# One fused attention and mixture-of-experts kernel: no zero products ahead of the last row tiles of the first expert, its routing's next phase begun earlier, and half of its first weights asked for later

## The chip, the cores and the metric

The kernel runs on one core of a Trainium2 chip. The time is that of one execution on the device in microseconds (us). TensorE (PE) multiplies, VectorE (DVE) and ScalarE (ACT) work element by element, GpSimd (POOL) issues the transfers that gather and scatter rows, and SyncE (SP) issues the other transfers. All engines run side by side, each its own instructions in a fixed order, with semaphores between them.

## The reference

```python
scores = scale * q @ k.T            # 8 batches x 8 heads, 576 positions, 64 wide
scores = where((rel >= 0) & (rel < 128), scores + bias, -1e9)   # bias: -slope[head] * |rel|
x = softmax(scores) @ v             # -> x [4608, 512]

logits = x @ w_gate                 # 8 experts, cap = 4608 / 8 = 576 rows each
for idx in argsort(-logits.flatten()):     # greedy, best first
    tok, e = idx // 8, idx % 8
    if assigned[tok] < 0 and counts[e] < cap:
        assigned[tok] = e; counts[e] += 1
out[rows of e] = relu(x[rows of e] @ w1[e]) @ w2[e]     # w1 512x1024, w2 1024x512
```

Everything is float32. The greedy assignment orders all 36,864 logits, so which rows an expert gets depends on which experts are full already.

## The kernel before

**Attention** runs first and writes `x` to DRAM. During its last part the router begins.

**The router** (class `Router`) finds the assignment in phases 0 to 7. In each phase the expert that fills up first is determined with its 576 rows, by counting logits over thresholds: VectorE builds indicator matrices (`ind`), TensorE counts (L597, `m`), and after three such steps the number of the expert (`ei`, or `guess` in phase 0) and its rows (`idx`) come out, the latter through products at L744 and VectorE's L753. A phase begins with the best expert that is left for each row (`first_choice`, L504 to L511) and the range of the logits (`ends`, L518 to L548, with TensorE at L523 and L530). In the profile the router's phase 0 has the line L457. Each phase is a generator that stops at points where other work may be placed between.

In phase 0 the first 256 rows of the first expert (row tiles 0 and 1, `idxa`) are found ahead of the other 320 (row tiles 2 to 4, `idx`).

**An expert** has two layers in 5 row tiles (4 of 128, one of 64). Float32 products are made from parts: every operand is split into a high part, by a cast, and a low part, the rest, and three products (high·high, high·low, low·high) are added. The weights of a layer come as 4 chunks of 512 KB (`raw`, four buffers; `loads`, SP's queue, L987, behind a load of the expert's number into a register, L984), and `split` makes of each the high part on ScalarE (L994) and the low part in two instructions on VectorE (L996). Chunk c holds the columns of hidden blocks 2c and 2c+1 in layer 1, and the rows of these blocks in layer 2. The rows are gathered by GpSimd (`gather`, L1006), transposed by TensorE into a PSUM bank (`turn`, L1030; the pool of `pg` has one bank), and read out by ScalarE (`xh`, L1033) and VectorE (`xl`, L1034). Layer 1 is L1054 (`ph`), with relu on ScalarE (`hh`, L1060) and the low part on VectorE (`hlo`, L1065); layer 2 is L1082, L1083 and L1085 (`po`), read out at L1089, and GpSimd writes the rows out (L1094, from three buffers).

**The first expert** is handled ahead of the loop over the experts, in `layer_moe`: rows 0 to 255 through layer 1 (part 0) and layer 2 (tiles 0 and 1), and then rows 256 to 575 are gathered and turned, ahead of which and between which `keep_warm` puts 16, 4 and 4 products of zeros (L1014, 128x512, onto an idle bank), with the transposes of tiles 3 and 4 in banks of the pool `po`. Then the loop begins, with part 1 of layer 1 for the first expert.

**What sets the order.** Each engine's instructions are ordered ahead of time by a scheduler: what stands earlier in the program goes first where both could, except where the program holds an instruction behind another (`issue_after`) or keeps a row of them in the order of the program (`keep_in_program_order`). Inside the loop `slot(k, i)` is called between pieces of layer work and does what is due there: a step of the router, a load (table `W_LOAD`), a split (`W_SPLIT`), and from i = 16 on the gather and the turns of the next expert's rows.

Of the kernel before, what the change touches and what calls it, by code (L numbers as in the profile page):

```python
# [5 lines left out]
F32 = mybir.dt.float32  # L6
F32R = mybir.dt.float32r
BF = mybir.dt.bfloat16
I32 = mybir.dt.int32
# [6 lines left out]
E, DM, F, N = 8, 512, 1024, 4608  # L16
# [402 lines left out]

CONST_AT = 4  # L420
WARM, WARM0, WARM1 = 11, 16, 4
EARLY = 4
AHEAD = (18, 0, 0)
EARLY0 = 1
WARM_A = 8
W_LOAD = [(0, 1, 0, 0), (0, 1, 1, 2), (0, 1, 2, 6), (0, 1, 3, 10),
          (1, 0, 0, 13), (1, 0, 1, 16), (1, 0, 2, 19), (1, 0, 3, 22), (1, 1, 0, 28)]
W_SPLIT = [(0, 1, 0, 2), (0, 1, 1, 6), (0, 1, 2, 10), (0, 1, 3, 14),
# [11 lines left out]
AHEAD_COLS, AHEAD_ROWS = 28, 256  # L440
# [535 lines left out]
class MoE:  # L976
# [61 lines left out]
    def layer1(self, w1, xg, part=None):  # L1038
        nc = self.nc
# [5 lines left out]
        cut = (0, 288, 576) if part is None else (0, AHEAD_ROWS, 576)  # L1045
        order = [(f, (0, 1) if part is None else (part,)) for f in range(8)]
        for f, ts in order:
            w = w1[f // 2].rearrange("p a (j f) -> p a j f", j=4)
            fo = (f % 2) * 128
            pp = {t: self.p["ps_h"].tile([128, 512], F32, name="ph")[:, 0:cut[t + 1] - cut[t]] for t in ts}  # L1050
            for j in range(4):
                for a, x in ((0, xh), (0, xl), (1, xh)):
                    for t in ts:
                        nc.tensor.matmul(pp[t], w[:, a, j, fo:fo + 128], x[:, j, cut[t]:cut[t + 1]],  # L1054
                                         start=(j == 0 and a == 0 and x is xh), stop=(j == 3 and a == 1))
                if j == 1 and part != 0:
                    yield
# [86 lines left out]

def layer_moe(tc, P, C, r, m, exact):
    ei = r.ei[0] if exact else r.guess
    g = m.gather(r.idx[0], range(2), None if exact else m.x[0:128 * AHEAD_COLS, :])
    raw = list(m.loads(ei, 0))
    if not exact:
        with tc.issue_after(r.ahead_pe.ins):  # L1150
            m.idle = P["ps_h"].tile([128, 512], F32, name="ph")
            for _ in range(WARM_A):
                tc.nc.tensor.matmul(m.idle, C["zero"][:, 0:128], C["zero"], start=True, stop=True)
    W = {(0, 0): [m.split(raw[0])]}
    for _ in m.turn(g):
        pass
    W[0, 0] += [m.split(raw[c]) for c in range(1, 4)]
    second = list(m.loads(ei, 1))
    W[0, 1] = []
    for i, _ in enumerate(m.layer1(W[0, 0], m.xg, 0)):  # L1160
        if i % 2:
            W[0, 1].append(m.split(second[i // 2]))
    for _ in m.layer2(W[0, 1], m.h, r.idx[0], ts=range(2)):
        pass
    route = (n for k in range(1, E) for n in r.phase(k, exact))
    g = m.gather(r.idx[0], range(2, 5))
    with tc.issue_after(r.last.ins):
        for _ in range(EARLY0):
            next(route)
    with tc.issue_after(r.last_pe.ins):  # L1170
        m.idle = P["ps_h"].tile([128, 512], F32, name="ph")
        m.keep_warm(WARM0)
    tn = m.turn(g, True)
    next(tn)
    with tc.issue_after(m.turned.ins):
        late = P["rt"].tile([1, 1], I32, name="late")
        last = tc.nc.vector.tensor_copy(late, r.guess[0:1, 0:1])
    for _ in tn:
        pass
    with tc.issue_after(last.ins):  # L1180
        for _ in range(EARLY - EARLY0):
            next(route)
    st = dict(wait=0, turn=0)
    raws, loaders = {(0, 1): second}, {}

    def slot(k, i):

        st["wait"] -= 1
        if st["wait"] <= 0 and (k + 1 not in r.idx or k + 2 not in r.idx and i >= AHEAD[min(k, 2)]):
            st["wait"] = next(route, 0)  # L1190
        for e, layer, c, due in W_LOAD:
            e += k
            if i >= due and e in r.ei and len(raws.get((e, layer), ())) == c:
                if c == 0:
                    loaders[e, layer] = m.loads(r.ei[e], layer)
                    raws[e, layer], W[e, layer] = [], []
                raws[e, layer].append(next(loaders[e, layer]))
# [14 lines left out]
    for k in range(E):  # L1212
        i = 0
# [98 lines left out]
```

## Time and profile before

| what | us |
|---|---|
| median of 3 runs (lowest to highest) | 706.08 (705.92 to 706.16) |
| profiled execution, its own time | 703.26 |
| its span, first to last instruction | 701.5 |
| TensorE busy | 666.6 |
| VectorE busy | 457.0 |
| ScalarE busy | 326.1 |
| GpSimd busy | 152.8 |

The median is 0.2 to 0.4% above the profiled execution, which is a single one. In the profile, times of the trace count from the span's start. The attention ends at about 205; the first expert's layer 1 begins at 223.26, the turn of its row tiles 2 to 4 stands between 248.50 and 255.38, and the second expert's rows are turned from 290.86 on. A row of the timeline has start, length, engine, line, operation, output and inputs, and in brackets the idle time of the engine before it and what ended it.

### The profile page before, as it was taken

The numbers are of one execution on the slowest core, as the hardware profiler recorded it, in microseconds if no ns is written. First come the engines' busy times: TensorE is split into PE (matmuls) and PEld (weight loads), VectorE is DVE, ScalarE is ACT, GpSimd is POOL, SyncE is SP. The second block draws the span as 40 slices with busy tenths as digits, with TensorE's granted clock in tenths as the row PEclk, the third lists the DMA queues.
The fourth block names the chain that finished last, engine by engine and source line by source line (L and its number), as shares of the span: only waits on it lengthen the run. The fifth ranks groups of instructions, "written<-read, shape, count | busy, mean of one in ns | idle before, by whom it ended". The sixth has DMA issues, their size and how long they took to land.

```text
span 701.5 us, 18916 instructions
## 1 busy us (share of the span) xinstructions
PE 666.6 (95%) x7290; PEld 583.9 (83%) x7292; DVE 457.0 (65%) x1902; ACT 326.1 (46%) x992; POOL 152.8 (22%) x337
## 2 busy tenths in 40 slices
PE   8999999999956999699999999999999999999996
PEld 5899889989854977489779879889988988988985
DVE  6778887887878848679679829837855625423210
ACT  6998898988844212524233234224314324423211
POOL 4122222122311201403223141132133023011011
PEclk9999999999985999999999999999999999999998
DMA  8475756566327102706327235135135334301001
GB/s 300 158 226 175 223 184 222 185 223 192 104 68 271 39 30 66 272 9 203 136 91 255 70 105 173 61 122 171 53 121 159 108 110 136 121 30 39 1 24 49
DMA packets 35139, 92.72 MB, mean 132 GB/s; under 512 B 3808, under 2 KB 13152, under 8 KB 35040
## 3 DMA queue, kind: packets, MB, share of 16 engines
q1 hardware_dynamic: 29152, 72.55, 31.9%
q0 software_dynamic: 5888, 18.88, 8.2%
q8 instruction: 59, 0.97, 0.6%
q14 instruction: 40, 0.33, 0.1%
HBM read 72.54 MB, written 18.87 MB: 130 GB/s over the span
## 4 chain that ended last, share of the span: by engine, by line
PE 84%; DVE 9%; DMA 3%; ACT 2%; issue 2%; POOL 0%; POOLq 0%; SPq 0%; DVEq 0%
PE ph L1054 27%; PE po L1082 10%; PE po L1083 9%; PE po L1085 7%; PE x L53 7%; PE s L53 7%; PE pt L53 6%; PE pt L160 6%; PE pg L1030 2%; DVE hl L996 1%; DMA g<-x,idx 1%; DMA g<-x,idxa 1%; PE ph L1014 1%; ACT u L147 1%; PE m L597 1%
## 5 line engine op out<-in xcount | busy, mean ns | idle before, releaser
L1054 PE MATMUL ph<-xh,hl 128*128 128x288 f32 (+2 forms) x1024 | 193.1, 300 | 1.6 <-ACT xh L1033 1.6
L1054 PEld LDWEIGHTS ph<-xh,hl 128*128 128x128 f32 x1024 | 155.9, 190 | 3.3 <-ACT xh L1033 2.4
L1082 PE MATMUL po<-hl,hh 128*128 128x512 f32 (+1 forms) x328 | 131.4, 401 | 0.0
L1083 PE MATMUL po<-hl,hh 128*128 128x512 f32 (+1 forms) x328 | 127.7, 389 | 0.0
L147 ACT ACTIVATE u<-u,mn 128x192 f32<-128x192 f32 (+2 forms) x288 | 124.1, 438 | 5.3 <-DVE mn L137 5.2
L1054 PE MATMUL ph<-xl,hl 128*128 128x288 f32 (+2 forms) x512 | 117.1, 298 | 0.0
L1060 ACT ACTIVATE hh<-ph 128x288 fp32r<-128x288 f32 (+2 forms) x128 | 46.8, 408 | 144.3 <-PE ph L1054 144.2
L1085 PE MATMUL po<-hl,hlo 128*128 128x512 f32 (+1 forms) x264 | 101.9, 386 | 0.0
L996 DVE TENSOR_TENSOR hl<-raw,hl 128x512 fp32r<-128x512 f32 x128 | 85.4, 682 | 10.9 <-ACT hl L994 10.5
L137 DVE CUSTOM_DVE_ANT_0 u<-s,bm 128x192 f32<-128x192 f32 (+1 forms) x248 | 71.8, 345 | 30.1 <-PE s L53 29.5
L1054 PEld LDWEIGHTS ph<-xl,hl 128*128 128x128 f32 x512 | 85.0, 190 | 0.1
L1034 DVE TENSOR_TENSOR xl<-pg,xh 128x512 fp32r<-128x512 f32 (+1 forms) x38 | 24.4, 641 | 92.4 <-ACT xh L1033 92.2
L1094 POOL DMA_INDIRECT out_dram<-o,idx x38 | 42.1, 1108 | 191.5 <-ACT o L1089 115.5
L994 ACT CAST hl<-raw 128x1024 fp32r<-128x1024 f32 x64 | 65.5, 1047 | 21.5 <-DMA raw<-in_w_dram 14.3
L1065 DVE SCALAR_TENSOR_TENSOR hlo<-ph,hh 128x288 fp32r<-128x288 f32 (+2 forms) x128 | 50.0, 416 | 38.7 <-ACT hh L1060 38.3
L1082 PEld LDWEIGHTS po<-hl,hh 128*128 128x128 f32 x328 | 62.3, 190 | 11.2
L1083 PEld LDWEIGHTS po<-hl,hh 128*128 128x128 f32 x328 | 62.3, 190 | 11.0
L1089 ACT COPY o<-po 128x512 f32<-128x512 f32 (+1 forms) x33 | 18.9, 574 | 104.3 <-PE po L1085 74.3
L53 PE MATMUL s<-qk 64*64 64x192 f32 (+1 forms) x992 | 59.8, 325 | 1.0 <-DVE mn L137 0.9
L1006 POOL DMA_INDIRECT g<-x,idx x38 | 41.5, 1093 | 78.7 <-PE pg L1030 29.1
L1085 PEld LDWEIGHTS po<-hl,hlo 128*128 128x128 f32 x264 | 49.6, 188 | 10.1
L147 ACT ACTIVATION_READ_ACCUMULATOR u<-u,mn 128x1 f32 x288 | 56.0, 194 | 0.0
(260 smaller groups left out, 952.8 us busy)
## 6 DMA issues: line engine op xcount, KB each, us to landing
raw<-in_w_dram SPq DMA_DIRECT2D x64, 512.0 KB, 4.4
qk<-in_qk_dram SPq DMA_DIRECT2D x32, 576.0 KB, 5.0
v<-in_v_dram SPq DMA_DIRECT2D x32, 288.0 KB, 3.6
x<-xb SPq DMA_DIRECT2D x14, 512.0 KB, 3.6
x<-xb SPq DMA_DIRECT2D x8, 128.0 KB, 3.4
x<-xb SPq DMA_DIRECT2D x4, 256.0 KB, 2.2
g<-x,idx POOLq DMA_INDIRECT x38, 3.5
out_dram<-o,idx POOLq DMA_INDIRECT x38, 2.8
```

The source lines that it names most:

```text
L53: put(nc.tensor.matmul(out, w, a, start=start, stop=stop, skip_group_check=True))
L137: put(nc.vector.tensor_tensor_reduce(out=weights(n, t, h), in0=x[:, c:c + 64 * m].rearrange("q (j k) -> q j k", k=64), in1=bm[n % NP][:, y ...
L147: put(nc.scalar.activation(u, u, AF.Exp, bias=st["mn"][:, i:i + 1], scale=-1.0, accum_out=st["sm"][:, i:i + 1]))
L994: self.last = nc.scalar.copy(hl[:, 0, :], raw)
L996: nc.vector.tensor_tensor(hl[:, 1, c:c + 512], raw[:, c:c + 512], hl[:, 0, c:c + 512].bitcast(F32), ALU.subtract)
L1054: nc.tensor.matmul(pp[t], w[:, a, j, fo:fo + 128], x[:, j, cut[t]:cut[t + 1]], start=(j == 0 and a == 0 and x is xh), stop=(j == 3 and a = ...
L1060: nc.scalar.activation(o, pp[t], AF.Relu)
L1065: nc.vector.scalar_tensor_tensor(d, pp[t][:, c0:c1], 0.0, o[:, c0:c1].bitcast(F32), ALU.max, ALU.subtract)
L1082: nc.tensor.matmul(out, a, wh, start=(f == 0), stop=False)
L1083: nc.tensor.matmul(out, a, wl, start=False, stop=(f == 7 and t == 4))
L1085: nc.tensor.matmul(out, hl[:, f, 128 * t:128 * t + 128], wh, start=False, stop=(f == 7))
L1094: self.sent = nc.gpsimd.indirect_dma_start(out=self.out, out_offset=bass.IndirectOffsetOnAxis(ap=idx[t][:r], axis=0), in_=o[:r, :], in_off ...
```

## The change

- `EARLY`, the number of steps of phase 1 of the router that are issued ahead of the loop, goes from 4 to 3, and these steps now stand at the very beginning of `layer_moe`, without the `issue_after` that held them back. The first four slots of the first expert hold the router's step behind the last layer-1 product (`last_mm`), and `WAIT_B = 2` lets the first slot in the loop pass without one.
- Only two (`SOON`) of the four chunks of the first expert's layer-1 weights are asked for ahead of the gather of the first rows. The other two, and all four of layer 2, are asked for behind a copy of the expert's number (`late`) that VectorE makes after the first row tile's low part. On SP the queue so has a wait for VectorE between the second and the third chunk.
- The products of zeros ahead of and between the turns of row tiles 2 to 4 are gone, and all three tiles use the one bank `pg`. The 8 products of zeros at the start of the first expert (`WARM_A`) stay.

```diff
-EARLY = 4
+EARLY = 3
 AHEAD = (18, 0, 0)
-EARLY0 = 1
-WARM_A = 8
+WAIT_B = 2
+SOON, WARM_A = 2, 8
...
-                        nc.tensor.matmul(pp[t], w[:, a, j, fo:fo + 128], x[:, j, cut[t]:cut[t + 1]],
+                        self.last_mm = nc.tensor.matmul(pp[t], w[:, a, j, fo:fo + 128], x[:, j, cut[t]:cut[t + 1]],
...
     ei = r.ei[0] if exact else r.guess
-    g = m.gather(r.idx[0], range(2), None if exact else m.x[0:128 * AHEAD_COLS, :])
-    raw = list(m.loads(ei, 0))
+    route = (n for k in range(1, E) for n in r.phase(k, exact))
+    for _ in range(EARLY):
+        next(route)
+    raw = list(m.loads(ei, 0, range(SOON)))
+    ga = m.gather(r.idx[0], range(2), None if exact else m.x[0:128 * AHEAD_COLS, :])
...
-    W = {(0, 0): [m.split(raw[0])]}
-    for _ in m.turn(g):
+    W = {(0, 0): [m.split(raw[0])], (0, 1): []}
+    tn = m.turn(ga)
+    next(tn)
+    with tc.issue_after(m.turned.ins):
+        late = P["rt"].tile([1, 1], I32, name="late")
+        tc.nc.vector.tensor_copy(late, ei[0:1, 0:1])
+    raw += list(m.loads(late, 0, range(SOON, 4)))
+    for _ in tn:
         pass
     W[0, 0] += [m.split(raw[c]) for c in range(1, 4)]
-    second = list(m.loads(ei, 1))
-    W[0, 1] = []
+    second = list(m.loads(late, 1))
...
+    gb = m.gather(r.idx[0], range(2, 5))
     for _ in m.layer2(W[0, 1], m.h, r.idx[0], ts=range(2)):
         pass
-    route = (n for k in range(1, E) for n in r.phase(k, exact))
-    g = m.gather(r.idx[0], range(2, 5))
-    with tc.issue_after(r.last.ins):
-        for _ in range(EARLY0):
-            next(route)
-    with tc.issue_after(r.last_pe.ins):
-        m.idle = P["ps_h"].tile([128, 512], F32, name="ph")
-        m.keep_warm(WARM0)
-    tn = m.turn(g, True)
-    next(tn)
-    with tc.issue_after(m.turned.ins):
-        late = P["rt"].tile([1, 1], I32, name="late")
-        last = tc.nc.vector.tensor_copy(late, r.guess[0:1, 0:1])
-    for _ in tn:
+    for _ in m.turn(gb):
         pass
-    with tc.issue_after(last.ins):
-        for _ in range(EARLY - EARLY0):
-            next(route)
-    st = dict(wait=0, turn=0)
+    st = dict(wait=WAIT_B, turn=0)
...
         if st["wait"] <= 0 and (k + 1 not in r.idx or k + 2 not in r.idx and i >= AHEAD[min(k, 2)]):
-            st["wait"] = next(route, 0)
+            if k == 0 and i < 4:
+                with tc.issue_after(m.last_mm.ins):
+                    st["wait"] = next(route, 0)
+            else:
+                st["wait"] = next(route, 0)
```

What this does to the order of the instructions is shown at three places. The first is VectorE from phase 0's row indices (`idx`) on: `pen` to `L_72` end phase 0, L504 to L511 are the first choice of phase 1, and `hl<-raw,hl` is the low part of a weight chunk. Before:

```order
L457 TENSOR_SCALAR pen<-Dc 128x8
L1065 SCALAR_TENSOR_TENSOR hlo<-ph,hh 128x256
L457 TENSOR_TENSOR base<-pen,Dc 128x8
L457 SCALAR_TENSOR_TENSOR left<-keyv,kmx,left 128x8
L457 TENSOR_TENSOR L_4863<-L_sb,pen 128x288
L457 SCALAR_TENSOR_TENSOR L_72<-T_4787,L_4863 128x288
L457 TENSOR_REDUCE ov<-Dc 128x1
L504 TENSOR_REDUCE b<-L_72 128x36
```

And now, from `L_4863` on:

```order
L457 TENSOR_TENSOR L_4863<-L_sb,pen 128x288
L996 TENSOR_TENSOR hl<-raw,hl 128x512
L457 SCALAR_TENSOR_TENSOR L_72<-T_4787,L_4863 128x288
L457 TENSOR_REDUCE ov<-Dc 128x1
L996 TENSOR_TENSOR hl<-raw,hl 128x512
L457 TENSOR_SCALAR ov<-ov 128x1
L504 TENSOR_REDUCE b<-L_72 128x36
L457 SCALAR_TENSOR_TENSOR ov<-kmx,ov 128x1
L1065 SCALAR_TENSOR_TENSOR hlo<-ph,hh 128x256
```

Before, no low part of a chunk of the first expert stood behind phase 0's `idx`; now two stand here, and four more stand behind L511, between the small rows of phase 1's `ends`.

The second place is TensorE between the last layer-2 product of row tile 1 and part 1 of layer 1. Before, its end (16 products of zeros, the transposes of tile 2 and 4 more products of zeros are ahead of these rows):

```order
L1030 MATMUL po<-ident_sb,g 128x128 x4
L1014 LDWEIGHTS zero
L1014 MATMUL ph<-zero 128x512
L1014 LDWEIGHTS zero
L1014 MATMUL ph<-zero 128x512
L1014 LDWEIGHTS zero
L1014 MATMUL ph<-zero 128x512
L1014 LDWEIGHTS zero
L1014 MATMUL ph<-zero 128x512
L1030 MATMUL po<-ident_sb,g 128x64 x4
L523 MATMUL m<-ident_sb,ext 1x128
L1054 MATMUL ph<-xh,hl 128x320 x4
```

Now, the whole of it:

```order
L1085 MATMUL po<-hl,hlo 128x512
L1030 MATMUL pg<-ident_sb,g 128x128 x8
L1030 MATMUL pg<-ident_sb,g 128x64 x4
L1054 MATMUL ph<-xh,hl 128x320 x4
L1054 MATMUL ph<-xl,hl 128x320
```

The products of zeros are gone, the transposes of the three tiles follow each other into one bank, and phase 1's transpose (L523) has moved up into layer 2 of tiles 0 and 1. The first count of phase 1 (L597) stands behind 15 products of part 1 of layer 1, before behind 43.

The third place is TensorE where the second expert's rows are turned (L1030), among the layer-2 products of row tiles 2 to 4 of the first. The third and the fourth of the five turns, before:

```order
L1082 MATMUL po<-hl,hh 128x512
L1030 MATMUL pg<-ident_sb,g 128x128 x4
L1083 MATMUL po<-hl,hh 128x512
L1030 MATMUL pg<-ident_sb,g 128x128 x4
L1054 MATMUL ph<-xh,hl 128x288
L1030 MATMUL pg<-ident_sb,g 128x128 x4
L1054 MATMUL ph<-xl,hl 128x288
```

And now:

```order
L1030 MATMUL pg<-ident_sb,g 128x128 x4
L1082 MATMUL po<-hl,hh 128x512
L1083 MATMUL po<-hl,hh 128x512
L1082 MATMUL po<-hl,hh 128x512
L1083 MATMUL po<-hl,hh 128x512
L1054 MATMUL ph<-xh,hl 128x288
L1030 MATMUL pg<-ident_sb,g 128x128 x4
L1054 MATMUL ph<-xl,hl 128x288
```

The first turn stood behind 51 of the 64 layer-2 products of tiles 2 to 4 and stands behind 35 now; from each turn to the next there were 12, 1 and 0 of them, and now there are 13, 12 and 4. L744, the products that give the second expert's row indices, stood behind 30 layer-2 products and stands behind 16.

## The prediction

> **What bounds the kernel now.** I read the page first (the clock row and the chain that ended last), then busy time by stage, then the chain of waits where the products of zeros stand, then the timelines of TensorE, VectorE and GpSimd around the two places that the change touches. From the page:
>
> ```profile
> PEclk9999999999985999999999999999999999999998
> PE 84%; DVE 9%; DMA 3%; ACT 2%; issue 2%; POOL 0%; POOLq 0%; SPq 0%; DVEq 0%
> ```
>
> TensorE (PE) carries 84% of the chain, and its clock drops in one place of the 40, slices 13 and 14: between the attention and the first expert. What the change can win must be idle or slow time of PE. The stages around the first expert follow; after the two times of each stretch come its length, then busy time and count for PE, PE's weight loads, VectorE (DVE), ScalarE (ACT) and GpSimd (POOL), then granted clock, DMA share and GB/s.
>
> ```profile
> 205.00:223.26 18.26, 8.05 (x75) 4.94 (x76) 15.68 (x61) 6.64 (x9) 2.23 (x2) 0.53 0.65 224
> 223.26:237.40 14.14, 14.14 (x120) 13.73 (x120) 12.54 (x41) 5.80 (x11) 0.00 (x0) 0.88 0.21 75
> 237.40:248.50 11.10, 11.06 (x50) 8.94 (x50) 5.17 (x20) 0.98 (x3) 3.82 (x4) 1.00 0.28 83
> 248.50:255.38 6.88, 6.59 (x37) 3.49 (x36) 1.66 (x5) 2.12 (x4) 0.98 (x1) 1.00 0.11 40
> 255.38:272.10 16.72, 16.72 (x125) 15.45 (x126) 12.50 (x69) 3.06 (x7) 0.00 (x0) 1.00 0.00 0
> 272.10:286.90 14.80, 13.69 (x77) 9.88 (x75) 14.04 (x52) 5.73 (x8) 5.76 (x6) 1.00 0.66 222
> 286.90:290.86 3.96, 0.00 (x1) 0.01 (x1) 1.88 (x8) 1.01 (x1) 3.05 (x4) 1.00 0.80 248
> 290.86:303.50 12.64, 9.77 (x47) 7.46 (x48) 9.09 (x27) 5.97 (x9) 2.50 (x3) 0.86 0.40 141
> ```
>
> They are: the search for the first expert's rows; layer 1 on rows 0 to 255; layer 2 on row tiles 0 and 1; the turn of row tiles 2 to 4 with its products of zeros; layer 1 on the other rows, without a gap; layer 2 on row tiles 2 to 4; a standstill of PE; the hand-over to the second expert. Beyond 303.5 the order of the program is the same, so I shift the rest as a whole. Three stretches can change length: up to 248.5, 248.5 to 255.38, and 272 to 303.5.
>
> **Part 1: two chunks behind the first rows.** The first rows' gather goes out at 213.55. On PE, and by the DMA issues:
>
> ```profile
> 218.95 1.11 PE L1030 MATMUL pg<-ident_sb,g 128*128 128x128 f32 x4 [2.12 <-DMA g<-x,idxa]
> 223.26 0.79 PE L1054 MATMUL ph<-xh,hl 128*128 128x256 f32 x2 [0.68 <-ACT xh L1033]
> raw<-in_w_dram SPq DMA_DIRECT2D x8, 512.0 KB, 4.4
> g<-x,idxa POOLq DMA_INDIRECT x2, 5.4
> g<-x,idx POOLq DMA_INDIRECT x3, 3.4
> ```
>
> The first gathers take 5.4 us among four weight chunks; three later ones, with no weights in flight, take 3.4. With two chunks ahead I take the 3.4: the transposes and the first layer-1 product come 2.0 us earlier, at about 221.3. The bounds are 0 (the two chunks left are still in the way) and 2.1 (the whole wait of 2.12). Two things take it back. The clock:
>
> ```profile
> 225.00:230.00 5.00, 5.00 (x38) 4.91 (x38) 3.95 (x16) 2.82 (x5) 0.00 (x0) 0.84 0.30 114
> 290.00:295.00 5.00, 4.14 (x13) 3.33 (x14) 2.19 (x6) 2.48 (x3) 1.94 (x2) 0.66 0.94 350
> 295.00:300.00 5.00, 2.55 (x14) 1.63 (x12) 3.40 (x10) 2.12 (x3) 0.88 (x1) 1.00 0.07 25
> ```
>
> A mean of 0.84 over 225 to 230 is half speed until 226.6. Unless it opens sooner, 2.0 us of earlier products are done at half speed and are worth 1.0 us: layer 1 ends at 236.4 instead of 237.4. Then VectorE:
>
> ```profile
> 237.38 0.67 DVE L996 TENSOR_TENSOR hl<-raw,hl 128x512 fp32r<-128x512 f32 x1
> 237.98 0.32 DVE L457 SCALAR_TENSOR_TENSOR idx<-ia 64x3 int32<-64x3 f32 x2
> 238.32 0.17 DVE L457 TENSOR_SCALAR pen<-Dc 128x8 f32<-128x8 f32 x1
> 242.38 0.31 DVE L511 TENSOR_TENSOR OH<-c_eb,am 128x288 bf16<-128x288 bf16 x1
> L996 DVE TENSOR_TENSOR hl<-raw,hl 128x512 fp32r<-128x512 f32 x16 | 10.9, 683 | 1.0 <-ACT hl L994 0.9
> ```
>
> Before, all splits of the weights are done by 238.05, ahead of layer 2. In the new order six of them (of layer-2 chunks 1 to 3) stand behind the row indices, among the first choice of phase 1. From the indices (238.30 less 1.0) VectorE has the rows from pen to OH, 242.69 - 238.32 = 4.4 us; six splits of 0.683, 4.1; and about 1.3 of layer 1's low halves and the small rows of the next search: 247.1. Nine products stand behind the last split, 0.227 us each (two rows below: starts 248.00 and 248.23): 249.1, against 248.5 now; as some of the 1.3 can hide in gaps I take **+0.3** for parts one to here. Bounds: -1.0, if no product waits for a split, and +3.3, the third rival's price.
>
> **Part 2: no products of zeros.** The chain of waits (start, length, what):
>
> ```profile
> 248.00 0.23 PE po L1083
> 248.23 0.23 PE po L1085
> 248.52 3.40 PE ph L1014 x15
> 251.93 0.44 PE pg L1030 x4
> 252.36 0.86 PE ph L1014 x4
> 253.66 0.86 PE ph L1014 x4
> 254.53 0.41 PE po L1030 x4
> 255.38 0.99 PE ph L1054 x5
> ```
>
> The zeros (L1014) hold 3.40 + 0.86 + 0.86 = 5.1 of the 6.88 us. Without them the transposes are no longer in turn over three banks but wait for the one bank pg, until ACT and DVE have read the tile before. What that takes is to be seen at the second expert, where one bank is used already:
>
> ```profile
> 290.86 0.66 PE L1030 MATMUL pg<-ident_sb,g 128*128 128x128 f32 x4 [3.97 <-DMA g<-x,idx]
> 298.19 0.63 PE L1030 MATMUL pg<-ident_sb,g 128*128 128x128 f32 x4 [1.66 <-issue]
> 299.49 0.40 PE L1054 MATMUL ph<-xh,hl 128*128 128x288 f32 x1 [0.68 <-ACT xh L1033]
> 300.27 0.66 PE L1030 MATMUL pg<-ident_sb,g 128*128 128x128 f32 x4 [0.38 <-DVE xl L1034]
> 302.53 0.46 PE L1030 MATMUL pg<-ident_sb,g 64*128 64x64 f32 x4 [0.16 <-DVE xl L1034]
> ```
>
> From tile to tile 300.27 - 298.19 = 2.08 us. Two such periods and 255.38 - 254.53 = 0.85 from the last transposes to the first product make 5.0 us instead of 6.88: **-1.9**. Bounds: -1.6 (the second period, 2.26, is used twice) and -2.5 (the transposes' 0.44 is hidden in each period). The rows themselves are there: gathers that go out at 238 to 241 and take 3.4 us. Layer 1 on the other rows starts 1.6 us earlier (+0.3 - 1.9).
>
> **Part 3: phase 1 begun ahead.** Its first choice and range are now done under layer 2 of tiles 0 and 1, so its first count (L597) stands behind 15 layer-1 products instead of 43. The rows:
>
> ```profile
> 262.37 0.42 PE L597 MATMUL m<-OHf,ind 128*128 128x16 bf16 x8
> 276.37 0.19 PE L708 MATMUL m<-ex,c_ones 128*128 128x36 bf16 x1 [0.94 <-DVE ex L701]
> 282.65 0.27 PE L523 MATMUL m<-ident_sb,ext 128*1 128x128 f32 x1 [0.16 <-DVE ia L750]
> 284.12 1.74 POOL L1006 DMA_INDIRECT g<-x,idx  x1 [2.68 <-issue]
> ```
>
> Before, the count came 262.37 - 255.38 = 7.0 us after the layer's start, 0.163 per product; 15 products make 2.4. So the count leads by 4.6 + 1.6 = 6.2 us, and if the search keeps its pace the second expert's gather goes out at 277.9 and its rows are back at 290.86 - 6.2 = 284.7. PE comes earlier too: the first transposes of the second expert stand behind 35 layer-2 products, before behind 51, so 16 x 0.227 = 3.6; with 1.6 for the earlier start and the waits of 0.94 and 0.16, which the lead covers, PE is there at 286.90 - 6.3 = 280.6 and waits 4.1 us, as long as now (3.97). The gain is in what lies around it. The two waits go, 1.1. Behind the first transposes PE now has 13, 12 and 4 products before the next ones, before 12, 1 and 0. A period of 2.08 is covered by 9 products, so the idle 1.66 + 0.68 + 0.38 + 0.16 = 2.88 us becomes about 0.4 before the first layer-1 product (299.49 - 298.19 = 1.30, of which 4 products cover 0.9) and 0.8 behind it (300.27 - 299.49), 1.2. Idle time goes from 1.1 + 3.97 + 2.88 = 7.95 to 4.1 + 1.2 = 5.3: **-2.6**. Bounds: -5.9, if the gather is not slowed (first rival), and +3.6 (last rival). The cold spell behind the standstill (0.66 over 290 to 295, a loss of 0.34 x 5 = 1.7 us) I keep as it is, since the standstill is as long. That POOL now issues five gathers before it writes an output tile costs nothing: three output tiles are buffered.
>
> **The sum.** +0.3 - 1.9 - 2.6 = -4.2 us. The profiled execution's own time is 703.26 (span 701.5 and 1.8 around it) and would become 699.1. The median of the runs is 706.08, 2.8 above it; I take the same difference off it: **701.9 us**.
>
> **The rivals.**
>
> *The gather comes back sooner.* Now it takes 290.86 - 284.12 = 6.7 us, in a stretch with a DMA share of 0.80; the other gathers take 3.4. Issued 6.2 us earlier it may meet fewer weight chunks. Then the wait of 4.1 becomes 0.8: 701.9 - 3.3 = 698.6. Against it: the same search also gives the expert's number, so its chunks are asked for earlier as well, and 272.1 to 286.9 already has a share of 0.66.
>
> *The turn goes cold.* Without zeros PE is busy in the 5.0 us of the turn for three transposes of tiles, 0.44 + 0.44 + 0.41 = 1.3 us. After 3.96 us of nothing the clock fell for 3.4 of the next 5 us; 2.55 busy of 5 (295 to 300) held it. 1.3 of 5 lies between them. If it falls, the first products of layer 1 lose 1.7 us: 701.9 + 1.7 = 703.6. The Trainium skill, "TensorE: Matmul & The Clock Gate", section "Part 4: PE-mode transpose", says that transposes do not count as busy in the same way; by it this rival would be the likely case. The trace is only partly with it: at 295 to 300 the clock stayed at 1.00, but products stood between the transposes.
>
> *The weights are late.* Layer-1 chunks 2 and 3 and all of layer 2 now wait for a copy on VectorE behind the first tile's low half and then for a free one of four buffers. If landing, cast and split run 3.3 us past my 247.1, to about 250.4, layer 2 of tiles 0 and 1 ends that much later: -4.2 + 3.3 = -0.9, 705.2. From 250 on it decides. Against it: a chunk takes 4.4 us, and layer 1, under which six of them must land, lasts 14 us.
>
> *The lead is lost* (slower). PE's new order is fixed, but phase 1 may gain nothing over PE: if its counts and searches queue on VectorE behind splits and low halves, only the 1.6 us remain. Rows are back at 289.3, PE arrives at 281.7 with its two waits kept, and stands 7.6 us instead of 3.97 (+3.6); the turns win 1.7 as above; a second stretch of 3.4 us at half clock costs 1.7. That is +3.6 in place of -2.6: 701.9 + 6.2 = 708.1. Break-even is at a lead of about 2 us instead of 6.2. Against it: VectorE is busy 14.04 of 14.80 us in the stretch from 272, so it is full there, but only 12.5 of 16.7 in layer 1 before it.
>
> **How the numbers follow.** Chances: forecast 0.50, sooner gather 0.15, cold turn 0.12, late weights 0.11, lost lead 0.12. The forecast's own range, with part 1 between -1.0 and +2.0 (beyond that it is the late weights) and part 2 between -2.5 and -1.6, is 700.0 to 703.9. The range 698.4 to 706.2 holds it, the cold turn, nearly all of the late weights and over half of the sooner gather, and leaves out some 2 in 10. A difference of 0.2%, 1.4 us, is what a measurement can tell from none: faster 0.50 + 0.15 + 0.12 = 0.77, same 0.11, slower 0.12.
>
> **What would show it.** Part 1: the wait for g<-x,idxa near 0 and the first layer-1 product near 221.3; the last split near 247. Part 2: from the last layer-2 product of tile 1 to the first L1054 of 320 columns 5.0 us, transposes 2.1 apart, clock 1.00 behind them. Part 3: L597 2.4 us behind that product, idx and the gather 6 us earlier, no wait at L708, one wait for g<-x,idx of about 4 us and little idle behind it. I am wrong if the gather returns in 3.4 us, if the clock falls at 254, or if a wait for hl stands in layer 2 of tiles 0 and 1 for more than 2 us.

## The result, and the profile after

The changed kernel takes 703.04 us (median of 7 runs, 700.84 to 704.69), the kernel before, run beside it, 706.16 (704.83 to 708.37): a ratio of 0.9946, 95% interval 0.9926 to 0.9967. The ratio is one of means: by it the changed kernel is 3.8 us faster, with an interval of 2.3 to 5.2, while the medians differ by 3.1. The forecast was 4.2 less, 701.9. The differences in us below are taken from the ratios.

The two profiled executions must be read with care. That of the changed kernel took 704.69 us, the longest of its runs, that of before 703.26, less than any of its seven. From the timelines of GpSimd, of before and of after, the first gather of the first expert:

```profile
213.55 1.18 POOL L1006 DMA_INDIRECT g<-x,idxa  x1 [13.53 <-DVE ind L457]
```

```profile
215.22 1.18 POOL L1006 DMA_INDIRECT g<-x,idxa  x1 [13.53 <-DVE ind L457]
```

The idle time of GpSimd ahead of it, 13.53 us, is the same in both, so the 1.67 us between the two were lost further ahead, in the attention, which the change doesn't touch. I compare the stages from this row on. The third expert's rows are turned at 338.61 before (125.06 behind the row) and at 337.81 after (122.59): 2.5 us gained in this pair, against 3.8 in the runs.

The stages after, as they were shown of before (start and end, length, busy time and count of PE, its weight loads, VectorE, ScalarE, GpSimd, then granted clock, DMA share, GB/s). They are layer 1 on rows 0 to 255, layer 2 on row tiles 0 and 1, the turn of row tiles 2 to 4, layer 1 on these, layer 2 on them up to the standstill, the standstill, and the hand-over to the second expert:

```profile
222.64:236.50 13.86, 13.86 (x117) 13.22 (x118) 10.15 (x37) 7.33 (x12) 0.00 (x0) 0.82 0.57 191
236.50:249.87 13.37, 13.35 (x66) 10.42 (x64) 12.94 (x52) 2.31 (x4) 3.40 (x4) 1.00 0.29 88
249.87:254.91 5.04, 1.71 (x13) 1.10 (x12) 2.65 (x8) 2.03 (x4) 1.47 (x2) 1.00 0.24 89
254.91:273.78 18.87, 18.14 (x126) 16.79 (x127) 11.66 (x59) 3.06 (x7) 1.94 (x3) 0.91 0.02 7
273.78:283.15 9.37, 9.37 (x58) 6.98 (x56) 9.26 (x30) 5.02 (x6) 2.56 (x1) 1.00 0.77 270
283.15:287.29 4.14, 0.00 (x1) 0.00 (x1) 0.95 (x4) 0.00 (x0) 3.23 (x4) 0.80 0.92 307
287.29:303.57 16.28, 14.95 (x68) 11.94 (x68) 12.62 (x38) 7.50 (x11) 3.87 (x5) 0.84 0.39 136
```

The turn (third row) lasts 5.04 us instead of 6.88, the standstill (sixth) 4.14 instead of 3.96. New is the clock: 0.91 in layer 1 behind the turn and 0.80 in the standstill, where it was 1.00 both times, and 0.84 in a hand-over that was 0.86, although PE now has work between the turns. In shorter stretches:

```profile
255.00:260.00 5.00, 5.00 (x30) 4.90 (x31) 1.08 (x7) 0.44 (x1) 0.00 (x0) 0.67 0.03 10
285.00:290.00 5.00, 2.71 (x9) 2.33 (x10) 0.94 (x3) 1.56 (x3) 3.82 (x4) 0.56 0.98 376
290.00:295.00 5.00, 5.00 (x20) 3.99 (x19) 3.22 (x10) 2.26 (x4) 0.77 (x1) 0.76 0.49 169
```

A stretch of 5 us with a mean of 0.67 is half clock for 0.33 x 10 = 3.3 us, right behind the turn; from the standstill on it is 0.44 x 10 + 0.24 x 10 = 6.8 us, before 3.4. The waits of PE where before had them, from its timeline:

```profile
218.79 0.66 PE L1030 MATMUL pg<-ident_sb,g 128*128 128x128 f32 x4 [0.31 <-DMA g<-x,idxa]
222.64 0.58 PE L1054 MATMUL ph<-xh,hl 128*128 128x256 f32 x1 [0.43 <-ACT xh L1033]
273.19 0.19 PE L708 MATMUL m<-ex,c_ones 128*128 128x36 bf16 x1 [0.73 <-DVE ex L701]
287.29 1.12 PE L1030 MATMUL pg<-ident_sb,g 128*128 128x128 f32 x4 [4.14 <-DMA g<-x,idx]
298.83 0.66 PE L1030 MATMUL pg<-ident_sb,g 128*128 128x128 f32 x4 [0.78 <-DVE xl L1034]
301.49 0.50 PE L1082 MATMUL po<-hl,hh 128*128 128x512 f32 x1 [0.55 <-ACT hh L1060]
```

The first gather is waited for 0.31 us (2.12 before), the second expert's 4.14 (3.97), and behind that 0.78 + 0.55 = 1.3 us are idle (2.9). The chain of waits around the turn (start, length, what):

```profile
251.93 0.67 PE pg L1030 x4
252.63 0.59 ACT xh L1033
253.24 0.70 DVE xl L1034
253.99 0.47 PE pg L1030 x4
254.49 0.38 ACT xh L1033
254.91 3.98 PE ph L1054 x15
258.90 0.27 PE m L597 x8
```

The turns are 253.99 - 251.93 = 2.06 us apart, bound by the one bank; L597 comes 258.90 - 254.91 = 3.99 us behind the first product.

By stages, this pair of executions differs as follows: up to the end of layer 2 on row tiles 0 and 1 by -0.3 us (34.65 instead of 34.91 behind the first gather), in the turn by -1.9, in layer 1 behind it by +2.2 (18.87 instead of 16.72), and from there to the third expert's first turn by -2.5 (64.03 instead of 66.51). That adds up to the 2.5 us gained. Of the 2.2 us lost in layer 1, half clock is 3.3 / 2 = 1.65; the wait at L708 now lies in this stage too.

### The profile page after: what moved, and what is told of

The parts are those of the page before. It is cut to its first block, busy times and chain, and to the rows that moved or that the text cites. A ratio compares the mean times of both kernels' runs of the same rounds, so it can differ in the third digit from the quotient of the medians.

```text
span 702.9 us, 18878 instructions
## 1 busy us (share of the span) xinstructions
PE 666.0 (95%) x7267; PEld 585.3 (83%) x7268; DVE 457.4 (65%) x1902; ACT 325.6 (46%) x992; POOL 150.6 (21%) x337
## 3 DMA queue, kind: packets, MB, share of 16 engines
HBM read 72.54 MB, written 18.87 MB: 130 GB/s over the span
## 4 chain that ended last, share of the span: by engine, by line
PE 78%; DVE 12%; ACT 3%; issue 3%; DMA 2%; POOL 0%; POOLq 0%; SPq 0%; ACTq 0%; DVEq 0%
PE ph L1054 26%; PE po L1082 8%; PE po L1083 8%; PE po L1085 7%; PE pt L53 6%; PE x L53 6%; PE s L53 6%; PE pt L160 6%; PE pg L1030 2%; DVE hl L996 2%; ACT u L147 2%; DMA g<-x,idx 1%; DVE hlo L1065 1%; PE m L597 1%; DVE xl L1034 1%
```

## The experiments

Ratios are to the kernel before, run beside each. "Parts" are those of the prediction: 1, two chunks behind the first rows; 2, no products of zeros and one bank; 3, phase 1 begun ahead.

### The three parts alone and in pairs

**Part 1 alone:** into the kernel before, only this.

```diff
+    raw = list(m.loads(ei, 0, range(2)))
     g = m.gather(r.idx[0], range(2), ...)
-    raw = list(m.loads(ei, 0))
...
+    with tc.issue_after(m.turned.ins):
+        late0 = ...; tc.nc.vector.tensor_copy(late0, ei[0:1, 0:1])
+    raw += list(m.loads(late0, 0, range(2, 4)))
...
-    second = list(m.loads(ei, 1))
+    second = list(m.loads(late0, 1))
```

> The kernel before with part 1 alone: two chunks of the first weights ahead of the first rows' gather, the rest behind the first tile's low half. Theory of the prediction (the parts add up): the first layer-1 product comes about 2 us sooner, and as nothing of phase 1 stands among the splits, the 1.0 us that this is worth at half clock stays: -1.0 us against before, first wait for g<-x,idxa near 0. Rival (late weights): a wait for hl in layer 2 of tiles 0 and 1 of over 1 us, and a time equal to before or +1. Rival (the clock decides): the first products run into the window grid differently, the gain is anything between 0 and -2 and the granted clock between 205 and 230 shows it.

Measured: 0.9967 (0.995 to 0.9985), -2.3 us, more than the 1.0 expected.

**Part 2 alone:**

```diff
-    with tc.issue_after(r.last_pe.ins):
-        m.idle = P["ps_h"].tile([128, 512], F32, name="ph")
-        m.keep_warm(WARM0)
-    tn = m.turn(g, True)
+    tn = m.turn(g)
```

> The kernel before without the 24 products of zeros and with one bank for all transposes (part 2 alone). The scheduler then also moves the router: the first count of phase 1 stands behind 27 layer-1 products instead of 43, and the second expert's turns behind 35, 48, 60 and 64 layer-2 products as in the changed kernel. Theory (the parts add up): the turn takes 5.0 us instead of 6.9, -1.9, and the hand-over about -0.7 (the turns are covered, but the gather's lead is 2 us smaller than in the changed kernel, so the wait for it is near 6 us): -2.6 in all. Rival (cold turn): in the executions in which the clock falls behind the turn 1.7 us are given back, the median is -1 to -2 and the runs spread by about 1.7 us more than those of before.

Measured: 0.9933 (0.9905 to 0.9962), -4.7 us; in its median (701.62) faster than all three parts together (703.04), though the two intervals overlap.

**Part 3 alone:** the changed kernel with parts 1 and 2 undone.

> The kernel before with phase 1 begun ahead (part 3 alone): all four chunks ahead of the gather, products of zeros kept. In its order the first count stands behind 15 layer-1 products, the second expert's turns behind 35, 48, 60 and 64 layer-2 products. Theory (the parts add up): -2.6 us, all of it between 270 and 304, with a wait for the second expert's gather of about 4 us; the turn as before, 6.9 us, clock 1.00 behind it. Rival (the lead is lost or never needed): since taking the zeros away already moves the turns in the order, part 3 adds nothing of its own; here that would show as a wait for g<-x,idx of 6 us or more and a time within 1 us of before.

Measured: 0.9994 (0.9979 to 1.001). The rival was right: no gain.

**Parts 1 and 3**, the zeros put back into the changed kernel:

```diff
+    last_pe = r.last_pe
...
+    with tc.issue_after(last_pe.ins):
+        m.idle = P["ps_h"].tile([128, 512], F32, name="ph")
+        m.keep_warm(16)
-    for _ in m.turn(gb):
+    for _ in m.turn(gb, True):
```

> The changed kernel with the 24 products of zeros and the banks of po for tiles 3 and 4 put back (part 2 undone). Theory (the parts add up): the turn takes 6.9 us again, so 1.9 us slower than the changed kernel in executions where that one's clock holds, -2.3 against before. Rival (cold turn): with the zeros the clock stays at 1.00 behind the turn in every execution, which gives back 1.7 us where the changed kernel's clock fell; then this kernel is the same as the changed one or up to 0.5 us slower, and its runs spread less.

Measured: 0.9968 (0.9947 to 0.9988), -2.3 us.

**Parts 2 and 3**, all four chunks ahead of the gather again:

> The changed kernel with all four chunks ahead of the first gather again (part 1 undone; parts 2 and 3). Theory (the second expert's gather collides with weight chunks): as in the two kernels with part 3 so far, three layer-2 chunks of the second expert are asked for together with its gather, whose first rows then take 6.7 to 8.5 us to land; -2 to -4 against before, slower than part 2 alone (-4.7). Rival (the parts add up): -4.7 and -0.4 make -5.1, and the gather lands in 5 us as in part 2 alone.

Measured: 0.9982 (0.996 to 1.0004), -1.3 us, not told from no change. The sum of the parts, -5.1, is excluded; the collision theory's -2 to -4 lies partly inside the interval.

**Parts 1 and 2**, without part 3:

> The kernel before with parts 1 and 2, without part 3: the changed kernel but for the router's phase 1, whose steps stand where they stood before. Additive theory: -2.3 (part 1 alone) and -4.7 (part 2 alone) make -7.0, about 699.7 where before is 706.7, and part 3 would then cost the changed kernel 3 us. Rival (both parts win the same wait): with part 2's order the second expert's gather is waited for anyway, so part 1's head start is spent in that wait; about -5, no faster than part 2 alone.

Measured: 0.991 (0.988 to 0.994), -6.4 us: some 2.6 us better than the changed kernel, at the edge of what the two intervals can tell.

Together, in us against before (each to between 1.1 and 2.1): part 1 -2.3, part 2 -4.7, part 3 -0.4; 1 and 2 -6.4, 1 and 3 -2.3, 2 and 3 -1.3; all three -3.8. Part 1 brings about 2 in every company (-2.3, -1.7, -1.9, -2.5). Parts 1 and 2 nearly add up. Part 3 is worth nothing where the zeros stay, and costs 2.6 to 3.4 where they are gone (each of these two to about 2.6).

Where part 3 costs shows at the second expert's first gather. It goes out 70.57 us behind the first expert's first one in before, 66.47 in part 2 alone, 66.04 in parts 1 and 2, and 65.37 in the changed kernel. So part 3 brings the gather forward by 0.7 us and no more, and the transposes that wait for it begin 6.7 us after its issue instead of 4.9. The contrast is clearest between parts 2 and 3 and parts 1 and 2 (which differ in part 1 as well). From GpSimd's timelines, parts 2 and 3, and then parts 1 and 2:

```profile
281.32 3.01 POOL L1006 DMA_INDIRECT g<-x,idx  x1 [7.95 <-PE m L523]
```

```profile
280.06 1.49 POOL L1006 DMA_INDIRECT g<-x,idx  x1 [6.88 <-PE m L523]
```

By the DMA issues of that time (issue to landing in the last column), the same two kernels:

```profile
g<-x,idx POOLq DMA_INDIRECT x1, 9.0
```

```profile
g<-x,idx POOLq DMA_INDIRECT x1, 4.8
```

And what PE waits for, by its list of waits:

```profile
PE pg L1030 <- DMA g<-x,idx: 6.5, 1, 6.5
```

```profile
PE pg L1030 <- DMA g<-x,idx: 2.3, 1, 2.3
```

In every kernel with part 3's order and its splits untouched, GpSimd took 3.00 or 3.01 us for the first gather, in those without it 1.15 to 1.74. With the weight chunks where the scheduler put them, the rows came 6.7 to 9.0 us after the issue with part 3 and 4.8 to 7.2 without it. In the changed kernel, which differs from parts 1 and 2 in part 3 alone, this is the row

```profile
280.59 3.01 POOL L1006 DMA_INDIRECT g<-x,idx  x1 [7.95 <-PE m L523]
```

with the transposes 6.7 us later, at 287.29, and a wait of 4.14 us instead of 2.3. Two causes were possible, the weight chunks that are asked for at the same time (three of layer 2, from 0.06 us behind the gather on; in parts 1 and 2 they are asked for from 0.67 us behind it on) and something that holds GpSimd itself. The next runs take them one by one.

### The weight chunks held back

Into the changed kernel:

```diff
+                if (e, layer) == (1, 1) and k == 0 and "late" not in st:
+                    continue
...
-                    loaders[e, layer] = m.loads(r.ei[e], layer)
+                    loaders[e, layer] = m.loads(st.get("late", r.ei[1]) if (e, layer) == (1, 1) else r.ei[e], layer)
...
                 next(gathers[k], None)
+                if k == 0 and "late" not in st:
+                    with tc.issue_after(m.turned.ins):
+                        st["late"] = P["rt"].tile([1, 1], I32, name="late1")
+                        tc.nc.vector.tensor_copy(st["late"], r.ei[1][0:1, 0:1])
```

> The changed kernel, in which the layer-2 chunks of the second expert are asked for behind a copy that VectorE makes after the first of its row tiles has been turned, that is behind all of its gathers' first rows; nothing else is changed. Theory (collision): the first gather lands 3.4 to 4 us after its issue instead of 6.7, TensorE stands still for 1 us at most instead of 4.1, and no or one window of half clock follows: 3 to 5.5 us faster than the changed kernel, 697.5 to 700. Rival (the gather is slow by itself, on GpSimd or in its descriptors): still 6 us or more, 703 as the changed kernel. A second rival: the chunks come late for the second expert's layer 2, and a wait for hl appears there.

Measured: 0.991 (0.9882 to 0.9938), -6.4 us, some 2.6 better than the changed kernel, again at the edge of what the intervals can tell. GpSimd's row, the DMA issue and PE's wait:

```profile
279.16 3.01 POOL L1006 DMA_INDIRECT g<-x,idx  x1 [7.97 <-PE m L523]
```

```profile
g<-x,idx POOLq DMA_INDIRECT x1, 5.5
PE pg L1030 <- DMA g<-x,idx: 3.0, 1, 3.0
```

The landing goes from 6.7 to 5.5, not to the 3.4 to 4 that were expected, and the time, 700.64, misses the 697.5 to 700 that were: the chunks were one cause, and 3.01 us on GpSimd are left. Behind the end of GpSimd's instruction it is now 5.5 - 3.0 = 2.5 us, with the chunks in flight 6.7 - 3.0 = 3.7 (changed kernel), 9.0 - 3.0 = 6.0 (parts 2 and 3) and 4.8 - 1.5 = 3.3 (parts 1 and 2).

### VectorE's splits held back too

The eight splits of the second expert's layer-1 chunks are kept behind its first turn as well (`issue_after` behind the same copy).

> The changed kernel with the second expert's layer-2 chunks held back as in the run before, and with all eight splits of its layer-1 weights on VectorE held behind its first turn too; before, six of them run on VectorE while GpSimd issues the gathers. Theory (VectorE's splits stretch GpSimd's first gather): that one takes 0.95 us as the later ones do, instead of 3.01, its rows land 3.4 to 3.7 us after the issue, and TensorE waits about 1 us instead of 3.0: 1 to 2.5 us faster than with the chunks alone held back, 698 to 699.5. Rival (the first gather behind a pause of GpSimd is slow in any case): it stays at 3.01 and the time is the same or, as the splits are late, slower.

Measured: 0.9927 (0.9906 to 0.9948), -5.2 us: no better than with the chunks alone held back, where 1 to 2.5 us more were expected. But the rows show what the splits do to the gather:

```profile
279.57 1.06 POOL L1006 DMA_INDIRECT g<-x,idx  x1 [7.46 <-PE po L1085]
```

```profile
g<-x,idx POOLq DMA_INDIRECT x1, 3.5
PE po L1082 <- ACT hh L1060: 1.5, 1, 1.5
PE pg L1030 <- DMA g<-x,idx: 1.2, 1, 1.2
```

The same first gather, behind a pause of about the same length (7.46 us instead of 7.95), takes 1.06 us when VectorE has only small rows to do. PE's wait falls to 1.2; the 1.5 us in the first row of waits, 0.5 with the chunks alone held back, are probably the price of the late splits. In the changed kernel VectorE had this in the 3.01 us:

```profile
280.65 0.67 DVE L996 TENSOR_TENSOR hl<-raw,hl 128x512 fp32r<-128x512 f32 x1
281.25 0.20 DVE L527 TENSOR_SCALAR ed<-ident_sb,em 1x1 f32<-1x1 f32 x1
281.38 1.27 DVE L996 TENSOR_TENSOR hl<-raw,hl 128x512 fp32r<-128x512 f32 x2
282.58 0.14 DVE L532 COPY ev<-m 128x1 f32<-128x1 f32 x1
282.65 0.67 DVE L996 TENSOR_TENSOR hl<-raw,hl 128x512 fp32r<-128x512 f32 x1
```

Splits without a pause of over 0.2 us between them. The traces of all 14 kernels bear the cause out: of their 560 gathers the 347 without a split beside them took 0.90 to 1.06 us on GpSimd, the 213 with one 0.90 to 3.01. The Trainium skill, "SBUF — State Buffer", section "SBUF: two separate sides", has the rule that VectorE and GpSimd share a pair of ports as an exclusive lock, which an operation of VectorE with two inputs from SBUF takes against a GpSimd operation that reads SBUF; the split (raw and hl) is such an operation, and the 3.01 against 1.06 us agree with the rule if the gather's instruction, whose indices lie in SBUF, counts as one that reads SBUF, which no run shows.

That splits follow each other closely is not enough for 3.01 us, however. In parts 1 and 2, where the gather (280.06, 1.49 us) was held for 0.4 us, they stand as close:

```profile
279.32 1.29 DVE L996 TENSOR_TENSOR hl<-raw,hl 128x512 fp32r<-128x512 f32 x2
280.73 0.67 DVE L996 TENSOR_TENSOR hl<-raw,hl 128x512 fp32r<-128x512 f32 x1
281.45 0.67 DVE L996 TENSOR_TENSOR hl<-raw,hl 128x512 fp32r<-128x512 f32 x1
```

What differs is the moment: this gather starts within a split, that of the changed kernel (280.59) in the gap of 0.12 us ahead of one. Whether that decides, and why a gather is held for about 2 us when one split takes 0.67, wasn't tried.

### The turn kept warm

Into the changed kernel, 6, 6 and 3 products of zeros behind the transposes of tiles 2, 3 and 4, which wait for the bank anyway:

```diff
-            if first and h % 3 != 2:
-                ps = self.p["ps_o"].tile([128, 512], F32, name="po")...
-            else:
-                ps = self.p["ps_g"].tile([128, 4, 128], F32, name="pg")
+            ps = self.p["ps_g"].tile([128, 4, 128], F32, name="pg")
...
-            if first and 1 < h < 4:
-                self.keep_warm(WARM1)
+            if first:
+                self.keep_warm(6 if h < 4 else 3)
...
-    for _ in m.turn(gb):
+    for _ in m.turn(gb, True):
```

> The changed kernel with 6, 6 and 3 products of zeros behind the transposes of row tiles 2, 3 and 4, in the time in which these wait for the one bank anyway; none ahead of the turn. Theory (cold turn): the turn keeps its 5.0 us within 0.3, the clock stays at 1.00 behind it, and the kernel is 1 to 2 us faster than the changed kernel in the executions in which that one's clock fell, about 701.7 in the median. Rival (the clock does not fall because of the turn, or the zeros stand in the way of the transposes): a turn of 6 us or more, or no difference.

Measured: 0.9952 (0.9933 to 0.9971), the same as the changed kernel, where 1 to 2 us were expected. The five microseconds behind the turn in this kernel:

```profile
253.70:258.70 5.00, 5.00 (x39) 4.49 (x38) 2.01 (x12) 0.75 (x3) 0.00 (x0) 1.00 0.07 22
```

The zeros do what they should: the turn stays at 5.04 us, and behind it the clock is 1.00 and PE does 39 products, where the changed kernel has 0.67 and 30 (its row 255 to 260 above). This holds without exception: of the 14 kernels profiled, the seven without products of zeros in the turn (the changed one and part 2, parts 1 and 2, parts 2 and 3 and three with the holds) fell to half clock right behind it, the seven with them didn't. But what is won there is lost at the standstill:

```profile
278.02 3.01 POOL L1006 DMA_INDIRECT g<-x,idx  x1 [7.96 <-PE m L523]
g<-x,idx POOLq DMA_INDIRECT x1, 8.1
PE pg L1030 <- DMA g<-x,idx: 5.5, 1, 5.5
```

The gather goes out earlier but lands 8.1 us after its issue instead of 6.7, and PE waits 5.5 us instead of 4.14.

**Chunks held back and the turn kept warm,** both in the changed kernel:

> The changed kernel with the second expert's layer-2 chunks held back and with 6, 6 and 3 hidden products of zeros in the turn of row tiles 2 to 4. Alone, the zeros kept the clock and won nothing, since TensorE then waited the longer for the gather. Theory (what is won ahead of the hand-over counts as far as the router's search moves with it): the first count comes about 1.1 us sooner, and so do idx and the gather; 1 us faster than with the chunks alone held back, about 699.6. Rival (the gather sets the end in any case): no difference, 700.6.

Measured: 0.9906 (0.9882 to 0.993), no difference from the hold alone (0.991), where 1 us was expected. The gather still took 3.0 us on GpSimd.

### Without part 3

**Parts 1 and 2, chunks held back:**

> The kernel before with parts 1 and 2 and the second expert's layer-2 chunks held back behind its first turn, without part 3. Theory (collision): the first gather, which takes 4.8 us among the chunks and 1.49 on GpSimd, lands in 3.5 to 4 us, and TensorE's wait of 2.3 us shrinks to about 1.2: 1 to 2 us faster than parts 1 and 2 alone, 699 to 700. Rival (the second chunk is late and matters already less here, since the first chunk is asked for 0.67 us behind the gather): same as parts 1 and 2 alone within 0.7 us.

Measured: 0.9901 (0.9871 to 0.9931), 698.8 us; parts 1 and 2 alone 701.16, which the intervals do not tell apart. PE's wait for the gather was 1.4 us instead of 2.3, near the 1.2 expected.

**The same with the turn kept warm:**

> The kernel before with parts 1 and 2, the second expert's layer-2 chunks held back behind its first turn, and 6, 6 and 3 hidden products of zeros in the turn of row tiles 2 to 4; phase 1 where it stood before. Theory (what is won ahead of the hand-over counts once the gather is quick): the clock stays at 1.00 behind the turn, 0.5 to 1.5 us faster than the same kernel without the zeros (698.8), 697.3 to 698.3. Rival (the search, and not TensorE, brings the second expert's rows): the wait for the gather grows by what was won, no difference; in the order, the second expert's turns now stand behind 45 to 64 layer-2 products instead of 35 to 64, with 7, 8, 4 between them, so that the turns may again be uncovered and the gain lost there.

Measured: 696.45 us, 0.9846 (0.9827 to 0.9866): 10.9 us faster than the kernel before, and faster than the changed kernel by a margin clear of both intervals. Against the kernel without the zeros it is 3.9 us by the ratios and 2.4 by the medians; 0.5 to 1.5 were expected. Its clock behind the turn and in the hand-over, GpSimd's first gather and two of PE's waits in the hand-over:

```profile
253.10:258.10 5.00, 5.00 (x35) 4.63 (x34) 4.62 (x24) 0.88 (x2) 0.00 (x0) 1.00 0.01 3
285.00:290.00 5.00, 4.78 (x30) 3.43 (x29) 4.69 (x20) 1.68 (x3) 1.94 (x2) 1.00 0.80 201
290.00:295.00 5.00, 3.45 (x29) 2.73 (x27) 3.65 (x12) 3.11 (x6) 0.93 (x1) 1.00 0.95 382
```

```profile
279.86 1.15 POOL L1006 DMA_INDIRECT g<-x,idx  x1 [0.30 <-PE po L1082]
```

```profile
PE pg L1030 <- DVE bq L927: 1.1, 1, 1.1
PE pg L1030 <- DMA g<-x,idx: 0.8, 1, 0.8
```

In steps of 5 us its clock stays at 1.00 from 230 to 690 us, while the kernel without the zeros has 0.66 behind the turn and 0.50 and 0.84 over 295 to 305; at half clock for some 10 us, that execution loses up to 5 us to it. PE's wait for the gather is 0.8 us. GpSimd here writes an output tile right ahead of the gather, which then took 1.15 us although splits stood beside it, and the first turn stands behind 45 layer-2 products instead of 35: the scheduler has ordered this kernel differently from the others, so whether the clock held in the hand-over by the zeros or by that order isn't told apart. (In the page of before, the clock drops in slices 12 and 13, which the prediction miscounted as 13 and 14.)

## Why the prediction was right, and where it was not

The direction, the size and the range held: -4.2 forecast, -3.8 measured (2.3 to 5.2). Several steps of the sum held in the profile, some nearly to the tenth: stage by stage it had +0.3, -1.9, 0 and -2.6, and the pair of executions shows -0.3, -1.9, +2.2 and -2.5. What did not hold is that part 3 brings the -2.6, and that the clock stays up behind the turn.

**Part 1, first rows.** Forecast: the wait of 2.12 us goes, the first product 2.0 us earlier. It went to 0.31, and the first product comes 222.64 - 215.22 = 7.42 us behind the gather's issue instead of 9.71: 2.3 earlier. Right.

**Part 1, what takes it back (+0.3).** From the gather's issue to the end of layer 2 of tiles 0 and 1 it is 249.87 - 215.22 = 34.65 us, before 248.46 - 213.55 = 34.91: -0.3 instead of +0.3, and no wait for hl. Part 1 by itself brings about 2 us in all four comparisons, and it was expected to bring 1.0. In its own profile this stretch is 33.52 us, -1.4. What the prediction let take it back, the first choice of phase 1 on VectorE among the splits, comes with part 3, though the prediction added it to part 1. In the profiles part 3 lengthens the stretch by 0.7 us (alone), 1.7 (beside part 1) and 1.5 (beside part 2), but not beside parts 1 and 2 (34.65 and 34.85), so that it takes back what part 1 wins is likely and not shown. Why part 1 alone brings 2.3 rather than the 1.0 expected isn't shown: its profiled execution was only 0.8 us ahead when it reached the second expert's first turn.

**Part 2, the turn (-1.9).** 5.04 us forecast as 5.0, against 6.88; the bank's period 2.06, forecast as 2.08. Right. The rival of the cold turn was priced right (1.7 us, half clock for 3.3 us) but its chance of 0.12 was wrong: the clock fell in seven of seven. A clock that falls at 254 was one of the prediction's own signs of being wrong, and it came: the 1.00 that the forecast had behind the turn failed. 1.7 us of PE busy time in 5.04 us (third row of the stages; the prediction had 1.3), nearly all transposes, did not hold the clock. The sentence of the Trainium skill ("TensorE: Matmul & The Clock Gate", section "Part 4: PE-mode transpose") that transposes do not count as busy in the same way was the better guide here than the row at 295 to 300, which had products among the transposes.

**Part 3, the wait of 4.1 us.** 4.14: right as a number. The lead was a little smaller (the gather's issue 284.12 - 213.55 = 70.57 us behind the first one before, 280.59 - 215.22 = 65.37 after: 5.2 instead of 6.2), since the cold turn delayed the first count (3.99 us behind the first product, 2.4 forecast); with the turn kept warm the count came after 2.2 us and the lead was 6.1. The idle time behind it is 1.3, forecast 1.2. The wait at L708 (0.73) stayed, which was to go.

**Part 3, "-2.6" and what it is due to: this step failed.** The interleaved turns behind 35, 48, 60 and 64 products come with part 2 as well as with part 3; the scheduler makes them as soon as either moves the count. So does most of the lead: 4.1 us in part 2 alone and 4.5 in parts 1 and 2, against 5.2 in the changed kernel. So most of what I booked on part 3 is had without it, and part 3's own share is nothing with the zeros (-0.4) and a loss of 2.6 to 3.4 without them. The assumption behind it, "if the search keeps its pace ... its rows are back", took 6.7 us from issue to landing as fixed. It isn't: it was 3.5 to 9.0 us in these kernels, and by the experiments what VectorE and SP do in that moment has a large share in it. With part 3 the first gather starts together with three weight chunks and at the head of a row of splits (3.01 us on GpSimd); in part 2 alone the order puts it so that 1.49 us do. The rival "the gather comes back sooner" named the weight chunks as the cause, and holding them back did win about 2.6 us (at the edge of what the intervals can tell), but it looked for the gain in the changed kernel, which had no less of them, and it didn't see the splits.

**The standstill's cold spell, kept as it was (1.7).** It doubled: 6.8 us of half clock instead of 3.4, of which 1.7 us fell into the standstill itself (0.20 x 4.14 x 2) and cost nothing. That leaves 5.1 us of half clock in which PE worked, 0.9 us more lost than booked; the hand-over as a whole gained as forecast all the same.

**Late weights, lost lead.** No wait for hl stood in layer 2 of tiles 0 and 1 of the changed kernel, and the lead was there (5.2 of 6.2 us). In parts 2 and 3, where PE waited 6.5 us, something like the lost lead is seen, but by a slower gather and not by a slower search.

That the total held is in part luck: the part that was booked with -2.6 brings nothing or costs, parts 1 and 2 bring more than was booked on them, and a cold turn that was left out of the sum took 1.7 back.

## What to carry to other kernels

Take the time from a gather's issue to its landing apart before you move it: how long the issuing engine is held, and what else is in flight. Moved by a few microseconds it may meet two-input VectorE operations and weight chunks, and give back more than the lead. Where PE waited for one bank anyway, products of zeros in that wait cost nothing here (the turn stayed at 5.04 us) and kept the clock; taking zeros out paid where they stood ahead of work that was ready. And book a gain on an edit only after trying it without the others: an edit here moved the order far from its own lines.

## What the runs showed of the hardware that was not expected

- GpSimd's instruction for an indirect gather of 128 rows, the second expert's first one, took 1.06 us with VectorE in small rows, and 1.15 to 1.74 or 3.01 with splits beside it that follow each other within about 0.2 us. In all 14 traces no gather without a split beside it took longer than 1.06.
- The rows of that gather landed 2.4 to 2.5 us after GpSimd's instruction ended where the second expert's layer-2 chunks were held back, and 3.3 to 6.0 us with chunks of 512 KB asked for around it.
- PE's clock fell to half after 5.04 us in which 1.71 us of transposes ran, and stayed at 1.00 with 15 products of zeros among them. It also fell behind an idle time much shorter than the standstill, in the hand-over of the changed kernel with the chunks held back and the turn kept warm:

```profile
296.00:301.00 5.00, 4.26 (x17) 3.62 (x17) 3.54 (x12) 2.70 (x4) 0.91 (x1) 0.66 0.27 84
PE pg L1030 <- DVE sat L611: 1.6, 1, 1.6
```

There the longest idle time ahead of the fall was 1.6 us, right ahead of transposes. In parts 1 and 2 the clock fell behind PE's wait of 2.3 us (0.66 over 285 to 290).
